# A gated mix of memory attention and a ReGLU block: the memory update in column tiles beside the recall denominators, with new planner lengths and a merged weight load

## The chip, the core and the metric

The kernel runs on one core of one Trainium2 chip. The metric is the device time of one execution, in microseconds (us). An execution has a span, from its first to its last instruction, and a little time around it.

## What is computed

The input x has 2048 rows of 512. Branch A is an attention with a compressive memory, in 32 heads of 16 columns and 4 segments of 512 rows; branch B is a gated linear block with 1792 hidden columns. A sigmoid gate of x mixes both. Cut to what matters here:

```python
g = sigmoid((x * gate_w).sum(-1, keepdims=True))
for s in range(4):                                    # segments of 512 rows
    qs, ks, vs = q[:, :, s], k[:, :, s], v[:, :, s]
    a_dot = softmax(qs @ ks.T * scale + causal_mask) @ vs
    pq = phi(qs)                                      # phi(t) = t + 1 if t > 0 else exp(t)
    a_mem = (pq @ M) / (pq @ z + 1e-6)                # recall: numerator and denominator
    o = sigmoid(beta) * a_mem + (1 - sigmoid(beta)) * a_dot
    pk = phi(ks)
    M, z = M + pk.T @ vs, z + pk.sum(rows)            # memory update, per head 16 x 16 and 16
a = concat(o) @ wo
b = (relu(x @ W_gate) * (x @ W_up)) @ W_down
out = g * a + (1 - g) * b
```

## The kernel before

All matmuls are in bf16 and go to PSUM: a pool S (L190) of one tile of four banks for the attention scores, and a pool G (L191) of four tiles of one bank for all else. Activations lie transposed, features on partitions; four chunks c of 128 features hold 8 heads each.

**Units of attention.** There are 16 units, one for each segment s and chunk c (`unit`, L698). A unit fills S with scores in row tiles of 32 (L716), ScalarE takes the exponential (L730), and GpSimd masks the diagonal blocks (L738). Then `rest` (L800) multiplies with V in tiles of 64 rows by 32 columns (pv, L818, two G tiles), recalls from the memory (rec), transposes both on VectorE (L853), scales, adds them on GpSimd (L895) and transposes back (L899) into oT.

**Dense work.** Projections for Q, K and V (`proj`), gate and up (`gu`, L627) and the down and output projections (`dn`, L647) are matmuls of 128 by 128 by 512 that go through `mm` (L236). `mm` issues one matmul, or four column tiles of 32 (L240) if the planner left the array in that mode.

**Memory.** phi(K) of a segment (`pk`) is transposed by four DMA transposes on SyncE's queue into pK (L566; pool pK has one buffer, so the next segment's transposes wait until the update has read it). `mz` (L596) forms the update of one chunk: 4 matmuls of 128 columns of weights by 136 (8 heads by 17, the 17th a column of ones, which gives z) into one G tile. Only the 8 diagonal blocks of 16 by 17 are wanted. VectorE adds the tile to mzacc (L611, L613), and GpSimd multiplies with the block mask bdm into M2 and Z2 (L618, L619). `mzs` (L917) plans four of these for each of the segments 0 to 2, after the projections of segment 0 and among the gate blocks of the others.

**Denominators.** `dens` (L756) is called at the first unit of the segments 1 to 3. Four column tiles multiply Z2 of the segment before with pq (den, L762) into one G tile. VectorE transposes it, GpSimd adds 1e-6, VectorE takes reciprocals (L779), GpSimd multiplies with the gates (L784, L786) and copies the result to CM (L792). R (L472) holds the exponential of the mixing gate, spread by 64 small GpSimd copies; RG (L477) is its product with the head gates.

**The planner.** No order is written by hand. Every piece of work is an `op` with a length for its engine, its dependences, a key (its due time), the buffers it takes and the ones it uses. `Sched.run` (L75) simulates the engines with these lengths and picks, engine by engine, what is ready and has the lowest key; a change of TensorE's tiling mode costs SW = 0.1 us, and a result is ready some 0.1 to 0.3 us after its end (LAT) unless the dependence names another delay. The instructions are then issued in that order, and each engine's order is fixed in the program. A length that is wrong does not break anything; it puts an engine in front of work that isn't ready, while the rest of its queue waits.

**Loads.** SyncE issues nearly all; at the start ScalarE's queue shares those of x and wq. wq comes in chunks: chunk 0 in two halves, then chunks 1 and 2 on SyncE and chunk 3 on ScalarE (L321), then wk, wv and the rest on SyncE.

Of the kernel before, what the change touches and what calls it, by code (L numbers as in the profile page):

```python
# [8 lines left out]
F32 = mybir.dt.float32  # L9
# [19 lines left out]
MM = 0.216  # L29
SW = 0.1  # L30


# [21 lines left out]
class Sched:  # L54
# [20 lines left out]
    def run(self):  # L75
# [5 lines left out]
        mode = "D"  # L81
        dma_free = 0.0
        cand = {e: [] for e in free}
        for o in self.ops:
# [5 lines left out]
        while len(order) < n:  # L90
            best = None
            for e, lst in cand.items():
                ests = []
                for o in lst:
                    t = max(free[e], o.ready)
                    ok = True
                    for b in o.alloc:
                        fr = b.pool.free
                        if not fr:
                            ok = False  # L100
                            break
                        t = max(t, min(fr)[0])
                    if ok:
                        ests.append((t, o))
                if not ests:
                    continue
                t0 = min(t for t, _ in ests)
                if e == "PE":
                    def pk(x):
                        t, o = x  # L110
                        k = o.key
                        if o.mode == "P":
                            k += -20.0 if mode == "R" else 4.0
                        elif o.mode == "D" and mode == "C" and not o.flex:
                            k += 3.0
                        return (k, o.seq)
                    pick = min((x for x in ests if x[0] <= t0 + 0.02), key=pk)
                else:
                    pick = min((x for x in ests if x[0] <= t0 + 0.02), key=lambda x: (x[1].cls, x[1].key, x[1].seq))
                t, o = pick  # L120
                if best is None or (t, o.cls, o.key) < best[0]:
                    best = ((t, o.cls, o.key), o, e, t)
# [12 lines left out]
            if o.land:  # L135
                dma_free = max(dma_free, t + 1.15) + o.land
                o.end = dma_free + 1.1
            for b in o.alloc:
                b.pool.free.sort()
                b.idx = b.pool.free.pop(0)[1]  # L140
# [19 lines left out]
def kernel(  # L160
# [39 lines left out]
    bdm = tl("bdm", [P, 8, DH], F32)  # L200
    mzacc = tl("mzacc", [P, NC, 8 * (DH + 1)], F32)
    M2 = [tl(f"M2_{i}", [P, NC, 8, DH]) for i in range(2)]
# [104 lines left out]
    for i in range(2):  # L307
# [6 lines left out]
        if i == 0:  # L314
            for eng, q, h in (("SP", nc.sync, 0), ("ACT", nc.scalar, 1)):
                def f(e, h=h, q=q):
                    cs = slice(256 * h, 256 * h + 256)
                    q.dma_start(out=wq_sb[:, 0, cs], in_=A_wq[0:P, cs])
                lwq.setdefault(0, []).append(load(f"wq0{h}", f, 65536, -299.5, eng=eng))
        else:  # L320
            for ci, eng, q in ((1, "SP", nc.sync), (2, "SP", nc.sync), (3, "ACT", nc.scalar)):  # L321
                def f(e, ci=ci, q=q):
                    q.dma_start(out=wq_sb[:, ci, :], in_=A_wq[ci * P:(ci + 1) * P, :])
                lwq[ci] = [load(f"wq{ci}", f, 131072, -298 + ci / 10, eng=eng)]

# [123 lines left out]
    for s in range(NSEG):  # L449
# [19 lines left out]
        for j in range(4):  # L469
            def f(e, s=s, j=j, cols=cols):  # L470
                for k in range(4):
                    nc.gpsimd.tensor_copy(R[s][32 * j:32 * j + 32, :, k], rcol[32 * k:32 * k + 32, cols])  # L472
            b.append(op(f"R{s}{j}", {"POOL": 0.8}, f, deps=[a], key=kz + 4, cls=2))

        def f(e, s=s):
            rv = R[s].rearrange("p t k -> p (t k)")
            nc.vector.tensor_tensor(  # L477
                RG[s % 2][:], HG[:, :, :, None].to_broadcast([P, NC, 2, 16]),
                rv[:, None, None, :].to_broadcast([P, NC, 2, 16]), ALU.mult)
        o_rg[s] = (b, f, kz)  # L480
# [61 lines left out]
    def proj_k(s, c):  # L542
# [15 lines left out]
        if s < NSEG - 1:  # L558
# [6 lines left out]
            def f(e):  # L565
                nc.sync.dma_start_transpose(out=pK[s].t[:, :, c * P:(c + 1) * P], in_=src.t[:])  # L566
            o_pKt[s, c] = op(f"pkt{s}{c}", {"SP": 0.1}, f, deps=[o_pk[s, c]], key=a.key, cls=0, land=0.8,
                             alloc=[pK[s]] if first else [], uses=[src] + ([] if first else [pK[s]]))

    def proj_v(s, t):  # L570
# [15 lines left out]
        for r in range(2):  # L586
            def f(e, r=r):
# [3 lines left out]
                    src[:, :, r, 0:DH])  # L591
            o_vs[s, t].append(op(f"vs{s}{t}{r}", {"POOL": 0.45}, f, deps=[o_v[s, t]] + (o_vs[s, t - 1] if t else []),
                                 key=a.key + 4, cls=2, alloc=[VS[s]] if t == 0 and r == 0 else [],
                                 uses=[Vp[s]] + ([] if t == 0 and r == 0 else [VS[s]])))

    def mz(s, c):  # L596
        g = Buf(G)

        def f(e):
            for t in range(4):  # L600
                nc.tensor.matmul(g.t[:, 0:8 * (DH + 1)], lhsT=pK[s].t[:, t, c * P:(c + 1) * P],  # L601
                                 rhs=Vp[s].t[:, t, 8 * c * HP:8 * (c + 1) * HP].rearrange(
                                     "p (h v) -> p h v", v=HP)[:, :, 0:DH + 1],
                                 start=(t == 0), stop=(t == 3))
        a = op(f"mz{s}{c}", {"PE": 4 * 0.06}, f, deps=[o_pKt[s, c]] + [o_v[s, t] for t in range(4)],
               key=dkey(1), mode="D", alloc=[g], uses=[pK[s], Vp[s]])

        def f(e):
            src = g.t[:, 0:8 * (DH + 1)]
            if s == 0:  # L610
                nc.vector.tensor_copy(mzacc[:, c, :], src)  # L611
            else:
                nc.vector.tensor_tensor(mzacc[:, c, :], mzacc[:, c, :], src, ALU.add)  # L613
        b = op(f"mza{s}{c}", {"DVE": 0.28}, f, deps=[a, o_mzacc[c]], key=a.key, cls=0, uses=[g])

        def f(e):
            mv = mzacc[:, c, :].rearrange("p (h v) -> p h v", v=DH + 1)
            nc.gpsimd.tensor_tensor(M2[s % 2][:, c, :, :], mv[:, :, 0:DH], bdm[:], ALU.mult)  # L618
            nc.gpsimd.tensor_tensor(Z2[s % 2][:, c, 0:8], mv[:, :, DH], bdm[:, :, 0], ALU.mult)  # L619
        prev = rec_of.get((s - 1, c))  # L620
        o_m2[s, c] = o_mzacc[c] = op(f"m2{s}{c}", {"POOL": 0.8}, f, deps=[b, o_bdm, prev, rec_of.get((s - 1, "den"))], key=a.key, cls=1)

# [130 lines left out]

    CM, o_cm = {}, {}

    def dens(s, k0, org):  # L756
# [3 lines left out]
        def f(e):  # L760
            for c in range(NC):
                nc.tensor.matmul(g.t[32 * c:32 * c + 32, :], lhsT=Z2[(s - 1) % 2][:, c, :], rhs=pq[s, c].t[:],  # L762
                                 start=True, stop=True, tile_position=(0, 32 * c))
        a = op(f"den{s}", {"PE": MM + 0.02}, f, deps=[o_pq[s, c] for c in range(NC)] + [o_m2[s - 1, c] for c in range(NC)],
               key=k0, mode="C", alloc=[g], uses=[pq[s, c] for c in range(NC)])
        rec_of[s, "den"] = a
        T = Buf(Tp)

# [4 lines left out]
        def f(e):  # L773
            nc.gpsimd.tensor_scalar(CMD[:, 0], T.t[:, :, 0:8], 1e-6, None, ALU.add)
        ad = op(f"dena{s}", {"POOL": 0.4}, f, deps=[a] + cmd_free, key=k0, uses=[T])
        rc = []
# [5 lines left out]
        def f(e):  # L782
            rv = R[s].rearrange("p t k -> p (t k)")
            nc.gpsimd.tensor_tensor(RGM[:], HGM[:, None, :].to_broadcast([P, 16, 8]),  # L784
                                    rv[:, :, None].to_broadcast([P, 16, 8]), ALU.mult)
            nc.gpsimd.tensor_tensor(CMD[:, 0], CMD[:, 1], RGM[:], ALU.mult)  # L786
        a = op(f"denm{s}", {"POOL": 0.8}, f, deps=rc + [org], key=k0 + 1)
        cmd_free.clear()
        for c in range(NC):
            def f(e, c=c):  # L790
                for j in range(4):
                    nc.gpsimd.tensor_copy(cm.t[32 * j:32 * j + 32, c, :, :], CMD[32 * c:32 * c + 32, 0, :, 2 * j:2 * j + 2])  # L792
            o = op(f"cm{s}{c}", {"POOL": 0.9}, f, deps=[a], key=k0 + c, cls=2, alloc=[cm] if c == 0 else [],
                   uses=[] if c == 0 else [cm])
# [5 lines left out]
    def rest(i, E, masks, behind):  # L800
# [4 lines left out]
        def f(e):  # L805
            for kb in range(8):
# [13 lines left out]
        a = op(f"pv{s}{c}", {"PE": 1.05}, f,  # L820
               deps=masks + [o_v[s, t] for t in range(4)] + [o for t in range(4) for o in o_vs[s, t]] +
               ([(behind, 0.0)] if behind else []),
# [14 lines left out]
        if c == 0:  # L837
            o_rg[s] = (op(f"RG{s}", {"DVE": 0.4}, frg, deps=b + [o_hg] + (attn_of_seg[s - 2] if s > 1 else []),
                          key=kz + 6, cls=2), None, None)
# [51 lines left out]
        if s > 0:  # L891
            Ob = outs[1][1]

            def f(e):
                (nc.vector if e == "DVE" else nc.gpsimd).tensor_tensor(Oa.t[:], Oa.t[:], Ob.t[:], ALU.add)  # L895
            deps = [op(f"ad{s}{c}", {"DVE": 0.5} if (s, c) == (NSEG - 1, NC - 1) else {"POOL": 1.18}, f, deps=outs[0][0] + outs[1][0], key=k0 + PU, uses=[Oa, Ob])]

# [19 lines left out]
    def mzs(s):  # L917
        for c in range(NC):
            mz(s, c)

# [68 lines left out]
```

The softmax here doesn't subtract the row's maximum and nothing guards it: scores larger than these inputs give would overflow.

## Time and profile before

| What | Value |
|---|---|
| Times of 3 runs | 1065.44, 271.23, 270.88 us; median 271.23 |
| Profiled execution | 271.66 us |
| Its span | 269.9 us |
| TensorE clock granted | 1.0 |
| ScalarE, VectorE, GpSimd busy | 72%, 69%, 70% of the span |
| Memory update matmuls (L601) | 48, first at 39.3, last at 144.4 us |
| Denominator matmuls (L762) | 12, at 67.4, 136.8 and 201.5 us |
| R copies (L472), CM copies (L792) | 64 of 220 ns, 48 of 237 ns |
| L774, L784, L786 on GpSimd | 532, 408, 676 ns each |
| Last unit's pv | 247.7 us; dense work alone after it |

The page and the answers of the trace name an instruction by its line in kernel.py, its engine and its operands: output, arrow, inputs. In a timeline the first column is the start in us from the start of the span, the second the time from the first start to the last end of the merged instructions, xN how many they are, and the bracket the idle time of the engine just before them and what ended it. A line of waits has the waiting engine and line, what it waited for, the total in us, how often, and the longest. PEld are TensorE's weight loads, SPq is SyncE's DMA queue. Matmuls are pipelined, so the start of one comes before the end that is shown of the one ahead of it.

### The profile page before, as it was taken

How to read it: one execution, taken by the hardware profiler on the slowest of the kernel's cores; microseconds unless marked ns; L12 is line 12 of the kernel's file. 1: busy time of each engine (PE TensorE's matmuls, PEld its weight loads, DVE VectorE, ACT ScalarE, POOL GpSimd, SP SyncE). 2: the span in 40 equal slices, each digit the busy share in tenths (PEclk: the TensorE clock that was granted, in tenths of full speed). 3: DMA queues.
4: the chain of work that ended last, by engine and by line, in shares of the span. 5: the costliest groups of instructions: out<-in, count | busy, mean ns of one | idle time of the engine just before them, and what ended most of it. 6: DMA issues, size and time to landing. Idle time of an engine off the chain costs nothing.

```text
span 269.9 us, 6743 instructions
## 1 busy us (share of the span) xinstructions
PE 262.2 (97%) x2658; PEld 117.2 (43%) x2658; DVE 185.9 (69%) x415; ACT 194.7 (72%) x189; POOL 188.7 (70%) x467
## 2 busy tenths in 40 slices
PE   8999999999999999999999999799999999999995
PEld 6433444344443434444445444244444444344444
DVE  1497888889995545889988845569986727366601
ACT  3598999999876576898887666588998575775110
POOL 9268889888689887579557988875878876535000
PEclk9999999999999999999999999999999999999999
DMA  6996990015800100000541010000000010000011
GB/s 173 291 255 176 324 246 4 0 22 128 89 5 19 41 19 2 2 0 2 134 82 22 22 41 21 0 2 0 2 2 1 2 43 19 21 2 2 0 39 41
DMA packets 27601, 15.52 MB, mean 57 GB/s; under 512 B 13617, under 2 KB 27569, under 8 KB 27569
## 3 DMA queue, kind: packets, MB, share of 16 engines
q1 hardware_dynamic: 26736, 14.63, 22.0%
q10 hardware_dynamic: 832, 0.46, 0.6%
q8 instruction: 21, 0.34, 0.5%
q14 instruction: 12, 0.09, 0.1%
HBM read 9.84 MB, written 2.10 MB: 44 GB/s over the span
## 4 chain that ended last, share of the span: by engine, by line
PE 83%; POOL 9%; DMA 3%; DVE 2%; issue 1%; ACT 1%; SPq 0%; POOLq 0%
PE G L242 66%; PE S L716 8%; PE G L818 6%; POOL E L738 5%; DMA wk_sb<-in_A_wk_dram 2%; PE G L240 2%; POOL R L472 1%; DMA xn<-in_A_x_dram 1%; POOL O L895 1%; POOL M L618 1%; ACT E L730 1%; PE G L601 1%; POOL CM L792 1%; DVE hT L641 0%; POOL Z L619 0%
## 5 line engine op out<-in xcount | busy, mean ns | idle before, releaser
L730 ACT ACTIVATE E<-S 128x2048 bf16<-128x2048 f32 x72 | 135.1, 1877 | 35.1 <-PE S L716 32.3
L738 POOL TENSOR_SCALAR_AFFINE_SELECT E<-E 64x256 bf16<-64x256 bf16 x256 | 114.0, 445 | 38.4 <-ACT E L730 24.0
L242 PE MATMUL G<-xT,wg_sb 128*128 128x512 bf16 x214 | 57.2, 380 | 1.9 <-DVE hT L641 1.9
L242 PE MATMUL G<-xT,wu_sb 128*128 128x512 bf16 x214 | 56.8, 380 | 0.0
L242 PE MATMUL G<-wd_sb,hT 128*128 128x512 bf16 (+1 forms) x238 | 54.4, 367 | 0.0
L641 DVE TENSOR_TENSOR hT<-G,rg 128x512 bf16<-128x512 f32 x56 | 37.6, 676 | 11.3 <-ACT rg L637 6.1
L853 DVE STREAM_TRANSPOSE T<-G 128x512 f32<-128x512 f32 x44 | 30.5, 704 | 15.5 <-PE G L818 12.9
L637 ACT ACTIVATE rg<-G 128x512 bf16<-128x512 f32 x56 | 32.5, 595 | 10.7 <-PE G L242 10.4
L242 PEld LDWEIGHTS <-hT 128*128 128x128 bf16 x238 | 21.8, 98 | 23.7 <-issue 2.6
L242 PEld LDWEIGHTS <-wg_sb 128*128 128x128 bf16 x214 | 19.1, 98 | 26.7 <-issue 6.7
L242 PEld LDWEIGHTS <-wu_sb 128*128 128x128 bf16 x214 | 19.6, 98 | 23.8 <-issue 1.9
L716 PE MATMUL S<-QT,K 32*128 32x192 bf16 (+7 forms) x512 | 28.6, 287 | 0.2
L716 PEld LDWEIGHTS <-K 32*128 32x128 bf16 x512 | 8.4, 92 | 29.8 <-issue 28.6
L899 DVE STREAM_TRANSPOSE oT<-O 128x512 bf16<-128x512 bf16 x16 | 11.3, 704 | 13.4 <-POOL O L895 13.4
L589 POOL COPY VS<-Vp 64x256 bf16<-64x256 bf16 x32 | 13.4, 418 | 8.7 <-DVE Vp L507 7.2
L818 PE MATMUL G<-E,Vp 64*32 64x128 bf16 (+7 forms) x512 | 19.1, 284 | 0.1
L818 PE MATMUL G<-E,VS 64*32 64x128 bf16 (+7 forms) x512 | 18.4, 284 | 0.4 <-DVE hT L641 0.4
L678 DVE TENSOR_SCALAR os<-G,ngcol 128x512 bf16<-128x512 f32 (+1 forms) x10 | 6.9, 688 | 16.3 <-PE G L242 16.3
L242 PE MATMUL G<-wo_sb,oT 128*128 128x512 bf16 (+1 forms) x68 | 17.3, 367 | 0.0
L242 PE MATMUL G<-xT,wk_sb 128*128 128x512 bf16 x64 | 16.3, 379 | 0.5 <-DMA wk_sb<-in_A_wk_dram 0.5
L472 POOL COPY R<-rcol 32x4 f32<-32x4 f32 x64 | 14.1, 220 | 3.0
L895 POOL TENSOR_TENSOR O<-O,O 128x512 bf16<-128x512 bf16 x11 | 12.8, 1164 | 4.0 <-DVE O L873 3.3
(90 smaller groups left out, 300.1 us busy)
## 6 DMA issues: line engine op xcount, KB each, us to landing
out_dram<-os SPq DMA_DIRECT2D x15, 128.0 KB, 1.7
wd_sb<-in_B_W_down_dram SPq DMA_DIRECT2D x1, 1792.0 KB, 12.7
xn<-in_A_x_dram SPq DMA_DIRECT2D x3, 512.0 KB, 4.3
wg_sb<-in_B_W_gate_dram SPq DMA_DIRECT2D x2, 512.0 KB, 5.0
wu_sb<-in_B_W_up_dram SPq DMA_DIRECT2D x2, 512.0 KB, 6.6
wg_sb<-in_B_W_gate_dram SPq DMA_DIRECT2D x3, 256.0 KB, 7.0
wu_sb<-in_B_W_up_dram SPq DMA_DIRECT2D x3, 256.0 KB, 7.0
wk_sb<-in_A_wk_dram SPq DMA_DIRECT2D x1, 512.0 KB, 5.9
```

Of the source, the lines that this page charges most:

```text
L242: nc.tensor.matmul(out_ap, lhsT=lhsT, rhs=rhs, start=start, stop=stop)
L472: nc.gpsimd.tensor_copy(R[s][32 * j:32 * j + 32, :, k], rcol[32 * k:32 * k + 32, cols])
L589: nc.gpsimd.tensor_copy(VS[s].t[64 * r:64 * r + 64, t, 0:H // 2 * HP].rearrange("p (h v) -> p h v", v=HP)[:, :, 0:DH], src[:, :, r, 0:DH])
L637: nc.scalar.activation(rg.t[:], g.t[:], ACT.Relu)
L641: nc.vector.tensor_tensor(h.t[:], u.t[:], rg.t[:], ALU.mult)
L716: nc.tensor.matmul(sp.t[:, j, off:off + w], lhsT=K2[s, cc].t[rows, kb, :, :].rearrange("p r k -> p (r k)"), rhs=QT[s, cc].t[rows, L - w:L] ...
L730: nc.scalar.activation(eb_.t[:], sp.t[:], ACT.Exp, scale=SCALE)
L738: nc.gpsimd.affine_select(out=v, in_=v, compare_op=ALU.is_ge, fill=0.0, base=0, pattern=[[0, 4], [1, 64]], channel_multiplier=-1)
L818: nc.tensor.matmul(gs[r].t[32 * j:32 * j + 32, L - w:L], lhsT=v, rhs=src.t[rows, j, off:off + w], start=(kb == 0), stop=(kb == 7), tile_po ...
L853: nc.vector.transpose(T.t[:].rearrange("p b e -> p (b e)"), g.t[:])
L895: (nc.vector if e == "DVE" else nc.gpsimd).tensor_tensor(Oa.t[:], Oa.t[:], Ob.t[:], ALU.add)
L899: nc.vector.transpose(dst.t[:], Oa.t[:].rearrange("p b r e -> p (b r e)"))
```

## The change

1. **Memory update.** `mz` becomes `mz_mm`: for each chunk c, row block t and column tile j a matmul of 32 columns of weights (two heads) by 34 (the same two heads by 17). All four chunks of a segment go into one G tile, 136 columns in all, and mzacc shrinks to that. Segment 0 has an op of its own in column mode (`mz0`); for the segments 1 and 2 the matmuls stand in the den op behind L762, which now also depends on the segment's four pK transposes and on V. One VectorE instruction per segment adds the tile to mzacc; the M2 and Z2 products spread two heads over the four column tiles by a repeated read.
2. **Planner.** Lengths of GpSimd work and of the SyncE transposes, a count of free buffers where one op takes several of one pool, a limit of eight loads on their way, and a margin MG of 1.0 us ahead of pv (from the masks), of RG (from the R copies) and of the transposes back in segments 1 to 3.
3. **R** is laid out [k, t] in place of [t, k], so that each copy writes four neighbours; its readers use other strides.
4. **wq.** Chunks 2 and 3 come in one load on ScalarE's queue.

```diff
+MG = 1.0
...
+                    need = {}
                     for b in o.alloc:
-                        fr = b.pool.free
-                        if not fr:
+                        fr, k = b.pool.free, need.get(b.pool, 0)
+                        if len(fr) <= k:
                             ok = False
                             break
-                        t = max(t, min(fr)[0])
+                        need[b.pool] = k + 1
+                        t = max(t, sorted(fr)[k][0])
+                    if ok and o.land and len(lanes) >= 8:
+                        t = max(t, lanes[-8])
...
-            for ci, eng, q in ((1, "SP", nc.sync), (2, "SP", nc.sync), (3, "ACT", nc.scalar)):
-                def f(e, ci=ci, q=q):
-                    q.dma_start(out=wq_sb[:, ci, :], in_=A_wq[ci * P:(ci + 1) * P, :])
+            for c0, c1, eng, q in ((1, 2, "SP", nc.sync), (2, 4, "ACT", nc.scalar)):
+                def f(e, c0=c0, c1=c1, q=q):
+                    q.dma_start(out=wq_sb[:, c0:c1, :], in_=A_wq[c0 * P:c1 * P, :].rearrange("(c p) n -> p c n", p=P))
...
-                    nc.gpsimd.tensor_copy(R[s][32 * j:32 * j + 32, :, k], rcol[32 * k:32 * k + 32, cols])
-            b.append(op(f"R{s}{j}", {"POOL": 0.8}, f, deps=[a], key=kz + 4, cls=2))
+                    nc.gpsimd.tensor_copy(R[s][32 * j:32 * j + 32, k, :], rcol[32 * k:32 * k + 32, cols])
+            b.append(op(f"R{s}{j}", {"POOL": 0.9}, f, deps=[a], key=kz + 4, cls=2))
...
-            o_pKt[s, c] = op(f"pkt{s}{c}", {"SP": 0.1}, f, deps=[o_pk[s, c]], key=a.key, cls=0, land=0.8,
+            o_pKt[s, c] = op(f"pkt{s}{c}", {"SP": 1.2}, f, deps=[o_pk[s, c]], key=a.key, cls=0, land=0.8,
...
+    W2 = 2 * (DH + 1)
+    def mz_mm(s, g):
+        for c in range(NC):
+            for t in range(4):
+                for j in range(4):
+                    h = 8 * c + 2 * j
+                    nc.tensor.matmul(g.t[32 * j:32 * j + 32, W2 * c:W2 * c + W2],
+                                     lhsT=pK[s].t[:, t, c * P + 32 * j:c * P + 32 * j + 32],
+                                     rhs=Vp[s].t[:, t, h * HP:(h + 2) * HP].rearrange("p (h v) -> p h v", v=HP)[:, :, 0:DH + 1],
+                                     start=(t == 0), stop=(t == 3), tile_position=(0, 32 * j))
...
+        b = op(f"mza{s}", {"DVE": 0.28}, f, deps=[a] + [o_mzacc[c] for c in range(NC)], key=key, cls=0, uses=[g])
...
+        a = op("mz0", {"PE": 0.5}, lambda e: mz_mm(0, g), deps=mz_deps(0), key=k, mode="C", alloc=[g], uses=[pK[0], Vp[0]])
...
+            if s < NSEG - 1:
+                mz_mm(s, gm)
+        gm, mds, mus = None, [], []
+        if s < NSEG - 1:
+            gm, mds, mus = Buf(G), mz_deps(s), [pK[s], Vp[s]]
+        a = op(f"den{s}", {"PE": MM + (0.5 if gm else 0.0)}, f,
+               deps=[o_pq[s, c] for c in range(NC)] + [o_m2[s - 1, c] for c in range(NC)] + mds,
+               key=k0, mode="C", alloc=[g] + ([gm] if gm else []), uses=[pq[s, c] for c in range(NC)] + mus)
...
-        ad = op(f"dena{s}", {"POOL": 0.4}, f, deps=[a] + cmd_free, key=k0, uses=[T])
+        ad = op(f"dena{s}", {"POOL": 0.62}, f, deps=[a] + cmd_free, key=k0, uses=[T])
...
-        a = op(f"denm{s}", {"POOL": 0.8}, f, deps=rc + [org], key=k0 + 1)
+        a = op(f"denm{s}", {"POOL": 1.1}, f, deps=rc + [org], key=k0 + 1)
...
-               deps=masks + [o_v[s, t] for t in range(4)] + [o for t in range(4) for o in o_vs[s, t]] +
+               deps=[(m, MG) for m in masks] + [o_v[s, t] for t in range(4)] + [o for t in range(4) for o in o_vs[s, t]] +
...
-            o_rg[s] = (op(f"RG{s}", {"DVE": 0.4}, frg, deps=b + [o_hg] + (attn_of_seg[s - 2] if s > 1 else []),
+            o_rg[s] = (op(f"RG{s}", {"DVE": 0.4}, frg, deps=[(x_, MG) for x_ in b] + [o_hg] + (attn_of_seg[s - 2] if s > 1 else []),
...
+        if s > 0:
+            deps = [(deps[0], MG)]
...
     def mzs(s):
-        for c in range(NC):
-            mz(s, c)
+        if s == 0:
+            mz0()
+        else:
+            mz_after(*gate_mz.pop())
```

The other planner lengths that change are those of the VS copies (0.45 to 0.5), the CM copies (0.9 to 1.06), the M2 and Z2 products (0.8 to 0.88) and the GpSimd sum of both attention parts (1.18 to 1.22).

## The prediction

> **What bounds the kernel now.** I read the page's busy line first, then TensorE's waits, then its timeline around the edited work, last the DMA queue's view of tile pK.
>
> ```profile
> PE 262.2 (97%) x2658; PEld 117.2 (43%) x2658; DVE 185.9 (69%) x415; ACT 194.7 (72%) x189; POOL 188.7 (70%) x467
> ```
>
> TensorE is busy for 262.2 of 269.9 us. No other engine is above 72%, so only two things shorten the span: less TensorE work, or fewer holes between its matmuls. The holes that the trace names are few:
>
> ```profile
> PE G L242 <- DVE hT L641: 1.9, 1, 1.9
> PE G L285 <- DVE mcole L262: 1.1, 1, 1.1
> PE G L242 <- DMA wk_sb<-in_A_wk_dram: 0.5, 1, 0.5
> PE G L818 <- DVE hT L641: 0.4, 1, 0.4
> PE G L601 <- DVE T L853: 0.2, 1, 0.2
> ```
>
> The L285 wait is the warm-up and isn't touched. Since the end of a matmul is modelled, I measure the other holes from start to start. In the timeline 14 dense matmuls run from 258.78 to 261.81, so a 512-column matmul takes 0.216 us. The four matmuls at 167.82 should be done at 168.69, and the next starts at 170.74: a hole of 2.05. A whole pv (L818) takes 1.10 elsewhere and 2.19 from 100.73 to 102.92: 1.09 lost. With 0.47 for wk these are 3.6 us.
>
> The edited work, TensorE's timeline:
>
> ```profile
> 74.13 0.24 PE L818 MATMUL G<-E,VS 64*32 64x128 bf16 x8
> 74.19 0.20 PE L818 MATMUL G<-E,Vp 64*32 64x64 bf16 x4
> 74.32 0.61 PE L242 MATMUL G<-xT,wu_sb 128*128 128x512 bf16 x2
> 74.76 0.41 PE L601 MATMUL G<-Vp,pK 128*128 128x136 bf16 x4
> 75.27 0.40 PE L716 MATMUL S<-QT,K 32*128 32x384 bf16 x8
> 75.60 0.68 PE L601 MATMUL G<-Vp,pK 128*128 128x136 bf16 x8
> 76.49 0.41 PE L601 MATMUL G<-Vp,pK 128*128 128x136 bf16 x4 [0.21 <-DVE T L853]
> 76.74 1.46 PE L242 MATMUL G<-wd_sb,hT 128*128 128x512 bf16 x6
> ```
>
> L601 is the memory update: 4 matmuls from 76.49 to 76.74 are 0.25 us, 62 ns each. The eight at 75.60 should end at 76.10, and the next waited until 76.49 for a PSUM buffer of pool G: 0.39 lost. The first two lines give the price of narrow matmuls on small tiles: eight start within 0.06 us, 7.5 ns each with their weight loads.
>
> What held TensorE at 170.74, timeline of all engines:
>
> ```profile
> 168.21 1.15 POOL L895 TENSOR_TENSOR O<-O,O 128x512 bf16<-128x512 bf16 x1
> ...
> 169.40 0.71 DVE L899 STREAM_TRANSPOSE oT<-O 128x512 bf16<-128x512 bf16 x1 [3.87 <-POOL O L895]
> 170.03 0.65 DVE L641 TENSOR_TENSOR hT<-G,rg 128x512 bf16<-128x512 f32 x1
> ...
> 170.74 1.02 PE L242 MATMUL G<-xT,wg_sb 128*128 128x512 bf16 x4 [1.90 <-DVE hT L641]
> ```
>
> VectorE stood 3.87 us in front of a transpose whose input POOL finished late. The ready hT product behind it kept its G buffer, and TensorE had none. At 100.6 it is the same: the timeline has VectorE 1.50 us before RG (L477) for POOL's R copies, two hT products behind it, and pv without its second G buffer.
>
> **What the Trainium skill says.** "TensorEngine Tiling (Array Packing)", Key Properties: changing the tiling mode drains TensorE. The trace agrees: two dense matmuls at 66.83 should end at 67.26, and den (L762), in column tiles, starts at 67.37: 0.11 per change. The same page, Instruction Overhead, charges some 60 cycles to each matmul, 25 ns at the 2.4 GHz that the next page gives. "TensorE: Matmul & The Clock Gate", Measured speedup vs the span model, has about 4 ns per tile on top of one duration. The trace's 7.5 ns lies between them, and I use it. "DMA: Bandwidth & Descriptors", Anatomy of one DMA, has about 2 us fixed per transfer; pK's transposes here take 2.4 at the least.
>
> **The change part by part.**
>
> *Memory update.* Removed: 48 matmuls by 62 ns, 3.0 us. Added: three blocks of 64 matmuls, 32 weight columns by 34. At 7.5 ns a block is 0.48; I take 0.50. The bounds are 0.30 (4 ns and some streaming) and 1.10 (17 ns, the mean over a whole pv, which streams far more). Two blocks follow den in its own mode and change nothing; the block of segment 0 adds one change, 0.11. The sum is 3.0 - 1.5 - 0.11 = 1.4 us less, with bounds +2.0 and -0.4. One G buffer per update instead of four also takes away the 0.39.
>
> *Off TensorE.* VectorE drains 3 times instead of 12: nine by 0.285 is 2.6 us less there. M2 and Z2 keep their element counts (497 and 288 ns); their input is now repeated along one axis, and R and RG have another layout at the same counts. I cost them at nothing: POOL and VectorE are 30% idle. If a POOL product grew by a fifth, 12 by 0.16 is 2 us of POOL, which shows only where VectorE waits for POOL.
>
> *The wait that is added.* den now needs all four pK transposes and V of its own segment, and TensorE's whole queue stands behind it. SyncE's timeline and tile pK:
>
> ```profile
> 66.08 2.52 SPq L566 DMA_TRANSPOSE pK<-pk  x2
> DMA to landing us min/median/max: 2.4/3.3/6.2
> ```
>
> The last transpose of segment 1 starts at 67.4 and lands at 69.8 to 72.9 by these, while den ran at 67.37. For segment 2 the last is issued at 140.8, and den ran at 136.78. So den must move about 3 to 8 us later. The planner knows this dependence, puts dense work first, and reckons 1.15 + 0.8 + 1.1 = 3.05 us per transpose. TensorE stands only for what is later than planned: nothing to 3.1 us in each of three places. I take 0.3 each (the timeline has one such wait, 0.3): 0.9. What den feeds is late next: its transpose, the reciprocals, POOL's CM, then VectorE's product L882. The first outputs of a segment wait for that, but their users (wo of the same segment) come tens of us later; only T buffers and VectorE's place in line are at stake. m2 of segment 1 is needed by den 2, some 60 us later.
>
> *Planner.* It had some POOL lengths short: denm 0.8 where rows show 408 + 676 ns, dena 0.4 for 532, R 0.8 for 4 x 220. It looked at one free buffer where pv takes two. It let a transpose or RG follow POOL with no margin. The edits (new lengths, the count of buffers, MG = 1.0 before pv, RG and the transpose) meet the two big holes directly: 2.05 + 1.09 = 3.1 us. A new order makes holes of its own; I keep two thirds of the gain, 2.1. If pv misses its place after a fill it pays one more mode change, 0.11; at 5 of 16 that is 0.5, which I count as well.
>
> *wq in one load.* On SyncE the second wq load stood 1.0 us until x had landed, and wk could be issued only at 4.14. With one transfer fewer ahead of it wk takes that earlier place, some 0.35 sooner. The bytes ahead of it are the same and may eat it; the last wq piece, twice as large, may be late by as much. Bounds +0.47 and -0.5; I take 0.2 gained.
>
> Sum: 1.4 + 0.39 + 2.1 + 0.2 - 0.9 - 0.5 = 2.7 us. The profiled execution took 271.66 (span 269.9 and 1.8 around it), so 269.0 of that kind; the median shown is 0.43 lower, 271.23, which gives **268.5 us**, 1.0% less.
>
> **Rivals.** (1) *The order heals all holes and blocks are cheap:* 2.0 + 0.39 + 3.1 + 0.47 = 6.0, 265.3. For it: each hole has an edit that names its cause. Against: a new order of 2,700 matmuls without a hole. (2) *The gain is spent:* blocks at 17 ns (loss 0.4) or new holes as large as the old: 270 to 272. (3) *Slower: den with the update in it becomes TensorE's wait.* Place: before L762 in segments 1 and 2 and before segment 0's update. The transposes stand in SyncE's queue behind the load of the next xT, which itself waited 3.4 us for TensorE in segment 2, and behind pk on VectorE. Lateness of 3.4 + 3.1 in segments 1 and 2 and 3.1 in segment 0 is 16 us, less the other gains of 3.6: 283 at the worst, 274 at half of it. It decides for slower once these waits pass 3.6 us, and for over 2% slower once they pass 9. For it: these landings spread by 3.8 us. Against: before, when the plan already put the update after its transposes by the same model, TensorE waited 0.3. (4) *The update does not overlap:* 25 ns a matmul, 1.6 us a block; 3.4 us worse than my term, 271.9. The pv rate speaks against it.
>
> **How the numbers follow.** My forecast with its own range of 266.4 to 270: 0.53. Rival 1: 0.10, of which 0.07 under 265.8. Rivals 2 and 4 together: 0.19. Rival 3: 0.18, of which 0.10 above 276.7. About 2% is what a measurement of this kernel can tell from no change, so faster 0.07, same 0.83, slower 0.10. The range reaches from 265.5 to 273.5: under it lies some 0.05 and over it some 0.14 (most of rival 3).
>
> **What would show it.** TensorE's busy time down by some 1.5 us; each block of 64 within 0.4 to 0.6 us; L762 moved to about 71 and 143; no wait of L242 on hT above 1 us; VectorE's waits on L895 shorter; the mzacc rows 3 instead of 12. Wrong if a block takes over 1 us, if TensorE shows waits on pK or at L762 of several us, or if holes of the old kind stand elsewhere with the same sum.

## The result and the profile after

The kernel after takes 267.44 us in the median, the one before 271.1. The ratio is 0.9865, with a 95% interval from 0.9846 to 0.9885: 1.4% less, some 3.7 us. It was forecast at 268.5, within 265.5 to 273.5. One of the four runs of the kernel before took 1065.44 us, the other three 270.88 to 271.23, and the median passes over it.

The page of the kernel after, its busy line:

```profile
PE 256.3 (96%) x2795; PEld 114.5 (43%) x2832; DVE 182.5 (69%) x404; ACT 195.3 (73%) x191; POOL 188.4 (71%) x467
```

TensorE's busy time fell by 5.9 us, more than the span, which fell from 269.9 to 265.7. Part of that is only missing records: the trace has 2832 weight loads, one for each matmul, but only 2795 matmuls, so 37 have no record. The same shows in TensorE's waits:

```profile
PE G L249 <- issue: 2.5, 16, 0.2
PE G L292 <- DVE mcole L269: 1.1, 1, 1.1
PE G L390 <- DMA xn<-in_A_x_dram: 0.4, 1, 0.4
PE G L852 <- issue: 0.4, 1, 0.4
PE S L411 <- DVE xT L398: 0.2, 1, 0.2
```

The 16 waits on "issue" of 0.2 us are not holes. They stand in front of groups that show an odd number of dense matmuls, where the planner issues them in pairs: one record of 0.216 us is missing each time. What is left in the dense part is the 0.4 inside a pv (0.5 from start to start). The waits for hT, for a transposed T and for wk are gone.

The memory update, TensorE's timeline of the kernel after:

```profile
77.26 1.04 PE L249 MATMUL G<-wd_sb,hT 128*128 128x512 bf16 x3
78.23 0.40 PE L787 MATMUL G<-pq,Z 128*32 128x512 bf16 x4
78.45 0.72 PE L613 MATMUL G<-Vp,pK 128*32 128x34 bf16 x64
79.00 1.92 PE L247 MATMUL G<-wd_sb,hT 128*32 128x512 bf16 x32
```

Sixty-four small matmuls take from 78.45 to 79.00, 0.55 us; the other two blocks take 0.52 and 0.54. That is 8.4 ns each with its weight load. den and its update start at 78.2 and 141.6, where den alone started at 67.4 and 136.8, and no wait stands in front of them.

VectorE and GpSimd at the place of the old hole of 2.05 us, timeline of the kernel after (L929 is the old L895, L936 the old L899, L665 the old L641):

```profile
166.84 0.83 POOL L481 COPY R<-rcol 32x4 f32<-32x4 f32 x4
...
167.65 0.72 DVE L887 STREAM_TRANSPOSE T<-G 128x512 f32<-128x512 f32 x1 [0.60 <-PE G L249]
...
167.76 1.15 POOL L929 TENSOR_TENSOR O<-O,O 128x512 bf16<-128x512 bf16 x1
...
168.29 0.65 DVE L665 TENSOR_TENSOR hT<-G,rg 128x512 bf16<-128x512 f32 x1
...
168.95 0.71 DVE L936 STREAM_TRANSPOSE oT<-O 128x512 bf16<-128x512 bf16 x1
```

Before, VectorE stood 3.87 us in front of this transpose with hT behind it. Now a T and the hT product come first, and the transpose starts at 168.95, 0.04 us after the sum has ended at 168.91. In VectorE's waits its total for this sum (all units) fell from 13.4 to 5.0 us.

### The profile page after: what moved, and what is told of

It reads as the page before. It is cut to its first block, busy times and chain, and to the rows that moved or that the text cites. A ratio compares the mean times of both kernels' runs of the same rounds, so it can differ in the third digit from the quotient of the medians.

```text
span 265.7 us, 7041 instructions
## 1 busy us (share of the span) xinstructions
PE 256.3 (96%) x2795; PEld 114.5 (43%) x2832; DVE 182.5 (69%) x404; ACT 195.3 (73%) x191; POOL 188.4 (71%) x467
## 4 chain that ended last, share of the span: by engine, by line
PE 95%; issue 2%; DMA 2%; SPq 0%; DVE 0%; DVEq 0%
PE G L249 74%; PE S L740 9%; PE G L852 7%; PE G L247 2%; DMA wq_sb<-in_A_wq_dram 2%; PE S L411 1%; PE G L613 1%; PE G L787 0%; SPq L317 0%; DVE os L702 0%; SPq L325 0%; PE G L390 0%; DVEq L702 0%
## 5 line engine op out<-in xcount | busy, mean ns | idle before, releaser
L762 POOL TENSOR_SCALAR_AFFINE_SELECT E<-E 64x256 bf16<-64x256 bf16 x256 | 116.2, 454 | 39.2 <-ACT E L754 25.4
L249 PE MATMUL G<-xT,wg_sb 128*128 128x512 bf16 x207 | 56.3, 380 | 1.1 <-issue 0.8
L665 DVE TENSOR_TENSOR hT<-G,rg 128x512 bf16<-128x512 f32 x56 | 38.2, 683 | 20.0 <-ACT rg L661 10.9
L249 PE MATMUL G<-wd_sb,hT 128*128 128x512 bf16 (+1 forms) x215 | 49.7, 366 | 1.3 <-issue 1.1
L249 PEld LDWEIGHTS <-hT 128*128 128x128 bf16 x226 | 20.5, 98 | 22.7 <-issue 3.0
L702 DVE TENSOR_SCALAR os<-G,ngcol 128x512 bf16<-128x512 f32 (+1 forms) x8 | 5.5, 683 | 21.1 <-PE G L249 21.0
L704 ACT ACTIVATE os<-G,ngcol 128x512 bf16<-128x512 f32 x9 | 6.2, 687 | 15.9 <-PE G L249 15.8
L907 DVE TENSOR_TENSOR O<-T,sm 128x256 bf16<-128x256 f32 x32 | 16.0, 529 | 0.3
```

Source lines behind the costliest of these rows:

```text
L249: nc.tensor.matmul(out_ap, lhsT=lhsT, rhs=rhs, start=start, stop=stop)
L665: nc.vector.tensor_tensor(h.t[:], u.t[:], rg.t[:], ALU.mult)
L704: nc.scalar.activation(ob.t[:, cs], g.t[:, 0:W], ACT.Copy, scale=ngcol[:, tt:tt + 1])
L762: nc.gpsimd.affine_select(out=v, in_=v, compare_op=ALU.is_ge, fill=0.0, base=0, pattern=[[0, 4], [1, 64]], channel_multiplier=-1)
L907: nc.vector.tensor_tensor(O.t[:, :, r, :], T.t[:, :, 0:DH], sm.t[:, r, :, None].to_broadcast([P, 16, DH]), ALU.mult)
```

## A sum that can be checked

Three things can be read off TensorE's timeline for every kernel: the update's matmuls, the number of mode changes (0.11 us each), and the holes, which I take from start to start beyond 0.216 us per 512 columns and beyond 0.11 at a mode change. Gaps of one whole missing record are left out. The "dense stretch" goes from the first wk matmul to the start of the last matmul. Each row is one profiled execution; ratios are those of the median times to the kernel before on the same chip, where it took 271.4 to 271.7 us beside the experiments. The runs are explained below.

| Kernel | Ratio (95%) | Dense stretch, us | Update | Mode changes | Holes | Rest |
|---|---|---|---|---|---|---|
| before | 1 | 256.4 | 3.0 | 163 | 3.6 | 231.8 |
| after | 0.9865 (0.9846 to 0.9885) | 252.4 | 1.6 | 170 | 0.5 | 231.6 |
| tiles_only | 0.9899 (0.9882 to 0.9916) | 253.1 | 1.6 | 166 | 1.5 | 231.7 |
| planner_only | 0.9902 (0.9882 to 0.9922) | 253.6 | 3.0 | 168 | 0.5 | 231.6 |
| lengths_only | 0.9893 (0.9871 to 0.9914) | 253.7 | 3.0 | 164 | 1.0 | 231.6 |
| margins_only | 0.9978 (0.9967 to 0.9988) | 255.9 | 3.0 | 165 | 3.0 | 231.8 |
| count_only | 1.0034 (1.0019 to 1.0050) | 257.2 | 3.0 | 167 | 3.9 | 231.9 |
| wq_only | 0.9986 (0.9972 to 1.0000) | 256.3 | 3.0 | 163 | 3.6 | 231.8 |
| copies_lengths | 0.9961 (0.9948 to 0.9974) | 255.2 | 3.0 | 163 | 2.5 | 231.7 |
| other_lengths | 0.9958 (0.9939 to 0.9977) | 255.1 | 3.0 | 163 | 2.4 | 231.7 |
| tiles_lengths_wq | 0.9853 (0.9832 to 0.9874) | 252.6 | 1.6 | 167 | 1.1 | 231.6 |
| after_no_margins | 0.9863 (0.9842 to 0.9884) | 252.7 | 1.6 | 171 | 0.8 | 231.5 |
| double_block | 0.9962 (0.9949 to 0.9975) | 254.8 | 3.2 | 170 | 1.5 | 231.5 |
| replanned_before | 1.0002 (0.9990 to 1.0015) | 256.1 | 3.0 | 164 | 3.0 | 232.1 |

The rest is what remains when all are taken off; it differs by 0.6 us over fourteen kernels, while the stretch differs by 4.9. So these three terms carry the change: from before to after 1.4 for the update, 3.1 for the holes and -0.8 for seven more mode changes. That makes 3.7; the stretch lost 4.0. The sum says where the time went, not what made the holes; that is what the experiments are for.

## The experiments

**tiles_only and planner_only: the change in two halves.**

Tiles_only is the kernel before with `mz` replaced by `mz_mm`, `mz0` and the den op that holds the update:

```diff
-    def mz(s, c):
...
+    def mz_mm(s, g):
...
+            if s < NSEG - 1:
+                mz_mm(s, gm)
```

Planner_only is the kernel before with all edits to `Sched.run`, the lengths and MG:

```diff
+MG = 1.0
...
+                        t = max(t, sorted(fr)[k][0])
...
-        a = op(f"denm{s}", {"POOL": 0.8}, f, deps=rc + [org], key=k0 + 1)
+        a = op(f"denm{s}", {"POOL": 1.1}, f, deps=rc + [org], key=k0 + 1)
```

> The kernel before with the column-tiled memory update alone, planned behind den as in the change; all other planner lengths, margins and loads as before. Theory A (TensorE's work and the holes add up): three blocks of 0.54 us in place of 3.03 us, one mode change more, no wait of the update for a G buffer: 1.3 to 1.7 us less than before, 269.4 to 269.8, and the holes behind POOL's R copies and its sum stay (some 3 us). Theory B (any new order is a new draw of holes): the time lies anywhere from 267 to 273 and the holes stand elsewhere. Theory C (den waits for pK): a wait of several us at L762.

> The kernel before with the planner's edits alone (GpSimd and SyncE lengths, margins, count of buffers, limit of loads); the memory update, the layout of R and wq as before. Theory A: the holes of 2.05 and 1.09 us go, some mode changes come: 1.8 to 2.8 us less, 268.3 to 269.3. Theory B: no more than a new draw, 269 to 273.

Measured: 268.76 and 268.68 us, ratios 0.9899 and 0.9902. Planner_only came as theory A had it. Tiles_only gained about 1 us more than theory A: the block price holds (1.6 in place of 3.0), but of the 3.6 us of holes only 1.5 stayed, where all but the update's own 0.7 should have. Its TensorE timeline has these two in place of the one of 2.05:

```profile
171.07 1.02 PE L242 MATMUL G<-xT,wg_sb 128*128 128x512 bf16 x4 [0.78 <-DVE T L876]
...
181.12 1.02 PE L242 MATMUL G<-xT,wq_sb 128*128 128x512 bf16 x4 [0.41 <-DVE T L876]
```

So the halves are not additive: each has 1.0% alone, both 1.4%. They share the holes. Why the tiles heal some of them with the old lengths isn't settled. VectorE has nine drains fewer and G three tiles fewer to give per segment, but the order is new too, and no run has the tiles in the old order. Theory B, a new draw of holes, covers this run: its range holds the time, and the holes stand elsewhere. Theory C fell: no wait at den.

**double_block: is the update's time on the path?**

```diff
             if s < NSEG - 1:
                 mz_mm(s, gm)
+                mz_mm(s, gm)
```

The op `mz0` of segment 0 is doubled in the same way.

> The kernel after with each memory update block of 64 matmuls issued twice (the second time it starts its sums anew, so the result is the same). Theory A: each block lies on the path that sets the end, 3 x 0.54 = 1.6 us more than after, 269.0. If another engine set the end there, or weight loads hid behind dense work, less than 0.8 more.

Measured: 270.52 us, ratio 0.9962 to before. Against after, by the quotient of the two ratios, it is 0.98% or 2.6 us. In the traces every engine has its instructions in the same order as in the kernel after, so nothing but the blocks differs. The dense stretch grew by 2.5, of which 1.6 are the blocks, as theory A had it, though its total of 1.6 was too small. The other 0.9 are holes: the one of 0.5 near 46 us takes 0.6, and a new one of 0.8 stands inside a doubled block:

```profile
79.89 1.25 PE L613 MATMUL G<-Vp,pK 128*32 128x34 bf16 x127
81.80 0.18 PE L613 MATMUL G<-Vp,pK 128*32 128x34 bf16 x1 [0.65 <-issue]
```

127 of the 128 matmuls run at the usual pace, and the last waits 0.65 us for nothing that the profile shows. The block is on the path at its full price. The last section comes back to the hole.

**replanned_before: is it luck of the order?**

```diff
-MM = 0.216
+MM = 0.2165
```

> The kernel before with the planner's length of a dense matmul at 0.2165 in place of 0.216, nothing else: the same work in a slightly different order. Theory A (the holes come from lengths that are wrong): within 1 us of before, 270.1 to 272.1, with holes behind POOL's sum and R copies again, perhaps at other places. Theory B (luck of the order): over 1 us away from before, on either side.

Measured: 271.58 us, ratio 1.0002. The hole behind POOL's sum is back at nearly the same work, from 169.6 to 171.15 (1.37 us idle, "DVE hT L641"), and pv loses 0.9 at 102, though here the trace names GpSimd's masks (0.4 in two waits) and not a G buffer. Theory A holds here: another draw with the old lengths leaves the time where it was and brings the larger hole back. It is one draw; tiles_only shows that a larger change of the work can move the holes.

**margins_only, lengths_only, count_only: which planner edit heals?**

Each is the kernel before with one kind of edit. Margins_only has MG in its three places, lengths_only all new lengths, count_only the count of buffers and the limit of loads; one line of each:

```diff
-               deps=masks + [o_v[s, t] for t in range(4)] + [o for t in range(4) for o in o_vs[s, t]] +
+               deps=[(m, MG) for m in masks] + [o_v[s, t] for t in range(4)] + [o for t in range(4) for o in o_vs[s, t]] +
...
-            o = op(f"cm{s}{c}", {"POOL": 0.9}, f, deps=[a], key=k0 + c, cls=2, alloc=[cm] if c == 0 else [],
+            o = op(f"cm{s}{c}", {"POOL": 1.06}, f, deps=[a], key=k0 + c, cls=2, alloc=[cm] if c == 0 else [],
...
-                        t = max(t, min(fr)[0])
+                        t = max(t, sorted(fr)[k][0])
```

> The kernel before with the margin of 1.0 us alone (ahead of pv, of RG and of the transposes back). Theory A (VectorE in front of late POOL work makes the holes, the margin moves it): the holes behind POOL's sum and R copies go, about 2.6 us; pv loses its place after a fill in some 5 of 16 units, 0.5 us; 2.1 us less than before, 269.0. Theory B (luck of the order): 269 to 272, holes of 1 to 3 us left.

> The kernel before with the new GpSimd and SyncE lengths alone. Theory A: R, dena and denm end where the plan has them, the hole at pv goes (0.6 us); the sum L895 was planned 1.18 for 1.16, so its hole stays: 0.3 to 1.0 us less, 270.1 to 270.8. Theory B: 269 to 272 with other holes.

> The kernel before with the count of free buffers and the limit of eight loads alone. Theory A: pv is planned behind its second G buffer, its hole of 0.6 us goes, the hole of 2.05 stays: 0.3 to 0.9 us less, 270.2 to 270.8. Theory B: 269 to 272 with other holes.

Measured: 271.14, 269.02 and 272.66 us; ratios 0.9978, 0.9893 and 1.0034. All three expectations of theory A failed. The lengths alone gain 1.1%, about 2.9 us, three times the most that I gave them; the margins gain 0.2%, where I gave them 2.1 us; the count loses 0.3%. Theory B, luck of the order, covers margins_only (3.0 us of holes left). TensorE's waits in count_only still have both holes:

```profile
PE G L248 <- DVE hT L647: 2.1, 1, 2.1
...
PE G L824 <- DVE hT L647: 0.7, 1, 0.7
```

In lengths_only, on the other hand, VectorE's waits for POOL shrink. Two lines of that view for the kernel before, then the same two for lengths_only:

```profile
DVE oT L899 <- POOL O L895: 13.4, 6, 3.9
...
DVE RG L477 <- POOL R L472: 4.0, 2, 2.5
```

```profile
DVE oT L899 <- POOL O L895: 5.2, 5, 2.0
...
DVE RG L477 <- POOL R L472: 1.9, 2, 1.2
```

I had expected the hole at the sum to stay in lengths_only, since the sum's own length was right (1.18 planned, 1.164 measured), and only a margin could move it. POOL's timeline of the kernel before, ahead of that sum, shows why that was wrong:

```profile
160.50 0.96 POOL L792 COPY CM<-CMD 32x32 f32<-32x32 f32 x4
161.53 1.41 POOL L738 TENSOR_SCALAR_AFFINE_SELECT E<-E 64x256 bf16<-64x256 bf16 x2
163.00 2.31 POOL L792 COPY CM<-CMD 32x32 f32<-32x32 f32 x8
165.35 0.87 POOL L472 COPY R<-rcol 32x4 f32<-32x4 f32 x4
166.29 1.84 POOL L738 TENSOR_SCALAR_AFFINE_SELECT E<-E 64x256 bf16<-64x256 bf16 x4
168.21 1.15 POOL L895 TENSOR_TENSOR O<-O,O 128x512 bf16<-128x512 bf16 x1
```

Three groups of CM copies, planned at 0.9 each, take 0.96 and 2.31 (1.16 each), and the R copies 0.87 for 0.8. These put POOL 0.64 us behind its plan before the sum begins. They aren't alone: the two masks at 161.53 take 1.41 where the plan has 0.95, another 0.46, and no edit changes that length. In order, a lateness adds up, and whoever waits at the end pays for all of it.

**copies_lengths and other_lengths: which lengths?**

Copies_lengths has the two lines below, other_lengths all the other lengths of lengths_only.

```diff
-            b.append(op(f"R{s}{j}", {"POOL": 0.8}, f, deps=[a], key=kz + 4, cls=2))
+            b.append(op(f"R{s}{j}", {"POOL": 0.9}, f, deps=[a], key=kz + 4, cls=2))
...
-            o = op(f"cm{s}{c}", {"POOL": 0.9}, f, deps=[a], key=k0 + c, cls=2, alloc=[cm] if c == 0 else [],
+            o = op(f"cm{s}{c}", {"POOL": 1.06}, f, deps=[a], key=k0 + c, cls=2, alloc=[cm] if c == 0 else [],
```

> The kernel before with the new lengths of the R copies (0.8 to 0.9) and the CM copies (0.9 to 1.06) alone. If these two made POOL late ahead of its sum, the hole of 2.05 and the one at pv go: 268.5 to 269.3, like all lengths together. If dena, denm and the others did, it stays at 271.

> The kernel before with the new lengths of all but the R and CM copies (dena, denm, VS, the sum, M2, SyncE's transposes). The counterpart: 271 if the copies made POOL late, 268.5 to 269.3 if these did; in between if both are needed.

Measured: 270.32 and 270.14 us, ratios 0.9961 and 0.9958. Each is in between: both are needed. Each leaves 2.4 to 2.5 us of holes, with the same two in TensorE's view (0.8 behind "DVE T L853", 0.6 behind "DVE hT L641"); together they leave 1.0. The other lengths hold SyncE's transposes (0.1 to 1.2) beside GpSimd's, and no run has those alone.

The traces of these two runs show how a length works, for they hold TensorE's order fixed: it issues its matmuls in both as in the kernel before. (In lengths_only one group of four has moved.) In copies_lengths VectorE's order differs by three hT products, each now ahead of a wait for POOL that it stood behind, and by one copy of Q that went to ScalarE. VectorE's timeline at the old hole, and its wait for R:

```profile
165.57 0.69 DVE L641 TENSOR_TENSOR hT<-G,rg 128x512 bf16<-128x512 f32 x1 [1.21 <-ACT rg L637]
168.01 0.71 DVE L899 STREAM_TRANSPOSE oT<-O 128x512 bf16<-128x512 bf16 x1 [1.75 <-POOL O L895]
168.65 0.67 DVE L853 STREAM_TRANSPOSE T<-G 128x512 f32<-128x512 f32 x1
```

```profile
DVE RG L477 <- POOL R L472: 6.7, 2, 3.6
```

In the kernel before, the hT product came behind this transpose, at 170.03. The wait for R has even grown, from 4.0 to 6.7 us, and still the pv at 99.8, for which it matters, takes 1.26 us where it took 2.19. So it isn't the length of the wait that costs; what costs is the ready work that stands behind it, and a longer length makes the planner put some of that work in front. This is a change of VectorE's order at fixed order of TensorE, so a lucky order of TensorE is no rival for it. Double_block aside, the five kernels with all new lengths have 0.5 to 1.1 us of holes, the two with a part 2.4 and 2.5, and of those with the old lengths all but tiles_only 3.0 to 3.9.

**wq_only.**

```diff
-            for ci, eng, q in ((1, "SP", nc.sync), (2, "SP", nc.sync), (3, "ACT", nc.scalar)):
+            for c0, c1, eng, q in ((1, 2, "SP", nc.sync), (2, 4, "ACT", nc.scalar)):
```

> The kernel before with chunks 2 and 3 of wq in one load on ScalarE's queue, nothing else. Theory A: wk is issued 0.35 us sooner and the first dense matmul starts that much earlier: 0.2 to 0.4 us less. Rival: the bytes ahead of wk are the same, so it lands when it did: within 0.1 us. The plan of what follows shifts a little too, which may hide either.

Measured: 271.41 us, ratio 0.9986 with an interval that reaches 1.0000. It agrees with 0.2 to 0.4 us and just so with nothing. SyncE's timeline of the kernel after has wk issued at 3.78 in place of 4.14, as expected. But the first wk matmul starts anywhere from 9.16 to 10.86 in the nine profiles with the old loads and from 9.78 to 10.63 in the five with the new. One profile of each can't show 0.3 us there. The traces of before and wq_only have the same order on every engine, and the dense stretch is as long in both (256.4 and 256.3), so whatever the load gains lies ahead of it.

**tiles_lengths_wq and after_no_margins: what do margins and count do in the end?**

Tiles_lengths_wq joins the edits of tiles_only, lengths_only and wq_only. After_no_margins is the kernel after with

```diff
-MG = 1.0
+MG = None
```

> The kernel before with the column-tiled update, the new lengths and the one wq load, without the margins, the count of buffers and the limit of loads. Theory A2 (the lengths heal the holes, margins and count only push pv out of its place): TensorE's order has pv after a fill in 13 of 16 units against 8 in the kernel after, 5 x 0.11 = 0.55 us; holes as few as after: 266.5 to 267.2, no slower than after. Theory A (margins and count do part of the healing): 1 to 2 us slower than after, 268.4 to 269.4.

> The kernel after with the margin MG replaced by the planner's usual delays. Theory A2: no difference beyond 0.5 us, 267.0 to 267.9 (pv after a fill in 8 of 16 units in both). Theory A: holes behind POOL's sum come back, 268.4 or more.

Measured: 267.46 and 267.44 us, ratios 0.9853 and 0.9863. Neither can be told from the kernel after, 0.9865. After_no_margins came as theory A2 had it. So margins, count and limit are not needed for the gain, and neither is the new layout of R, which tiles_lengths_wq lacks; no run has that layout alone. Tiles_lengths_wq was to be 0.3 to 0.9 us faster than after; the three mode changes that it saves (167 against 170) are spent on a hole of 0.59 at 179. No run beats the kernel after by more than its interval.

## Why the prediction was right

*The forecast* of 1.0% less was near the 1.4% measured, and its mechanism held: TensorE stayed the bound, with less work and fewer holes. The sum missed by 1.0 us (2.7 for 3.7), and 0.9 of it is the wait that was feared at den. Part of the nearness is luck: tiles_only and planner_only show that the terms don't add up one by one, and two of the three planner edits that it trusted bring little or nothing alone.

*Memory update.* 0.50 us a block forecast, 0.54 measured; 1.4 us gained forecast, 1.3 with the extra mode change. The price came from eight narrow matmuls of pv in the old trace, and the double block shows that it is paid on the path. The estimate of 25 ns per matmul in rival 4, worked out from the 60 cycles of the Trainium skill's tiling page ("TensorEngine Tiling (Array Packing)", Instruction Overhead), is three times too high for this stream, 8.4 ns. Four tiles take turns in it, so one tile still has only one matmul in 34 ns.

*The update's G buffer.* 0.39 forecast; gone. Two short waits of a fill behind L601 (0.15 and 0.14) that I had not counted went with it, which makes 0.7.

*The wait that was added.* 0.9 us of loss forecast, none measured. den moved later by 10.9 us in segment 1 and 4.8 in segment 2, where I had said 3 to 8; the planner put dense work in front. Rival 3 is refuted for this order: no wait at L787 or L613. Its own figure was off: half of its 16 us, less 3.6, gives 275.6, not 274. The landing at 72.9 takes the 5.5 us that were the longest in segment 1; the 6.2 of the line shown would give 73.6.

*The planner.* 2.1 us forecast from a new order that keeps two thirds of 3.1. Of the 3.1 us of holes that went by the table 0.7 are the update's, so 2.4 are the planner's: both big holes went, in planner_only and in the kernel after, and new ones of 0.5 came. The prediction had named three edits that "meet the two big holes directly", lengths, count and margin. Alone, only the first does: the lengths gain 2.9 us, the margin 0.6, and the count loses 0.9. A margin covers up to 1.0 us at one place; the lengths cover what adds up ahead of it. One reading was wrong: of the 1.09 us that pv lost, not all is the missing G buffer.

```profile
101.54 0.40 PE L818 MATMUL G<-E,VS 64*32 64x512 bf16 x8 [0.41 <-DVE hT L641]
...
102.64 0.26 PE L818 MATMUL G<-E,Vp 64*32 64x192 bf16 x8
```

Some 0.8 us stand in front of 101.54, behind hT, and 0.3 in front of 102.64, where the weight load waits on "issue". The last section comes back to those.

*Mode changes.* 0.5 forecast for pv out of its place, 0.66 measured (six besides mz0's). The program of the kernel after has 8 pv not directly behind a fill, against 1. I had laid that to the margin; after_no_margins has the 8 as well, tiles_lengths_wq, without count and limit, 3, and count_only 4 against 2 in margins_only. It is the count of free buffers or the limit of loads, which no run separates, that moves pv more.

*wq.* 0.2 forecast, 0.4 measured with an interval from 0 to 0.8: not settled.

*Rivals.* Rival 1 (all holes go, cheap blocks) came nearest in mechanism: the holes did go. It was 265.3 because it left out the mode changes and took the block at 0.30. Rival 2 and rival 4 are refuted by the table and the block.

## What to carry to other kernels

Where a planner fixes each engine's order, compare its lengths with the trace's rows for every small operation, not only for the one at the hole: here copies planned 0.06 to 0.26 us too short, several in a row, had a share in a hole two engines further on, and longer lengths healed it better than a margin did. A hole on the bounding engine can belong to the order of another: GpSimd was late, VectorE stood in front of it with ready work behind, and TensorE lacked the buffer that this work held. Ask first what could go ahead of the wait. Price narrow matmuls from a burst of narrow ones in the old trace, and try such a price by issuing the block twice.

## What was not expected of the hardware

TensorE has holes of 0.2 to 0.8 us among short instructions that no wait in the traces explains, and several fall at the same count of its instructions, though not at the same work. Two of them, in the kernel after and in double_block:

```profile
46.41 0.19 PE L852 MATMUL G<-E,Vp 64*32 64x64 bf16 x1 [0.35 <-issue]
```

```profile
46.75 0.18 PE L740 MATMUL S<-QT,K 32*128 32x64 bf16 x1 [0.48 <-issue]
```

The kernels after, tiles_only, tiles_lengths_wq and after_no_margins have one near 46 us inside pv. In double_block, which issues 64 matmuls more ahead of it, it stands inside the fill before pv. In all five, 477 or 478 weight loads were recorded before it. Double_block has its next one after 990. In before, margins_only, count_only and wq_only one of 0.3 stands inside pv near 102 us, after 1017; copies_lengths and other_lengths have less than 0.1 at that count. Where 478 falls among long dense matmuls, as in the kernel before, there is none. The count isn't all: lengths_only and planner_only pass 1017 inside a pv without a hole. What TensorE waits for there isn't shown, and no run tried it.
